# Moving the third reading of a VectorE exponential to GpSimd in a multi-query attention kernel, with a fourth buffer set and a new packing

## The chip, the cores and the metric

The kernel runs on one core of one Trainium2 chip. The metric is the device time of one execution in microseconds (us), the median of several. The engines are called PE (TensorE), ACT (ScalarE), DVE (VectorE) and POOL (GpSimd), as the profile has them; "spacing" is the time from one instruction's start to the next one's, and a "record" is the profile's own duration of one instruction. A tile is written as partitions x columns.

## The reference, cut to what matters

```python
S, D, H, Dh, F = 2048, 640, 32, 20, 1728          # bf16
xn = layernorm(x)
q = (xn @ wq) as 32 heads;  k = xn @ wk;  v = xn @ wv     # one k and one v for all heads
p = softmax(q k^T / sqrt(Dh));  o = p v
out = x + o @ wo + silu(xn @ w1) @ w2
```

The costly part is the exponential: 32 heads x 2048 x 2048 scores, which are 2048 blocks of 128 x 512.

Of the kernel before, what the change touches and what calls it, by code (L numbers as in the profile page):

```python
# [46 lines left out]
NZ = 3  # L47
ZB = 3
ZWAIT = 6
SWITCH = 0.105  # L50
S_LEAD = 0.56
PV_PRESS = 12
DVE_TH = 3.0
U_PRIO = 0.9
X_PRIO = 1.6
# [287 lines left out]
class Builder:  # L343
# [17 lines left out]
    def alloc(self):  # L361
        sb = self.sb
        self.ps = self.stack.enter_context(self.nc.psum_tensor("psall", [P, 8 * BANK], F32))
        self.xnT = sb([P, DC, S], BF16)
        self.w1 = sb([P, DC, F], BF16)
        self.w2 = sb([P, FC, D], BF16)
        self.wq = sb([P, DC, D], BF16)
        self.wqp = sb([P, DC, 2 * P], BF16)
        self.qd = sb([P, 2, QW], BF16)
        self.wo = sb([P, DC, D], BF16)  # L370
        self.kv_st = sb([P, 2, DC, DH], BF16)
        self.wk = sb([P, DC, P], BF16)
        self.kT = sb([P, 2, S], BF16)
        self.v = sb([P, 5, KT, SLOT], BF16)
        self.qT = sb([P, HT, 2, QW], BF16)
        self.E = sb([P, NBLK * QW], BF16)
        self.Z = sb([P, NZ, ZB * QW], I16)
        self.Y = sb([P, NZ, 2, ZB * QW], I16)
        self.U = sb([P, 2, QW], BF16)
        self.stk = sb([P, 64], BF16)  # L380
        self.UT = sb([P, 2, 4, P], BF16)
        self.W = sb([P, 4, 3, DH + 1], F32)
        self.hT = sb([P, FC, QW], BF16)
        self.o = sb([P, 2, 4, D], BF16)
        self.oT = sb([P, DC, QW], BF16)
        self.tb = sb([P, 2, QW], BF16)
        self.xres = sb([P, 4, D], BF16)
        self.yx = self.w1[:, :, :].rearrange("p a b -> p (a b)")[:, 0:8 * D].bitcast(F32).rearrange(
            "p (i e) -> p i e", i=4)
        self.ost = sb([P, 3, D], BF16)  # L390
        self.idf = self.w2[:, 4, 0:2 * P].bitcast(F32)
        self.idb = sb([P, P], BF16)
        self.st6 = sb([P, NT, 2, 6], F32)
        self.mv = sb([P, NT, 2], F32)
        self.rstd = sb([P, NT], F32)
        self.nb = sb([P, NT], F32)
        self.ex2 = sb([P, NT], F32)
        self.junk = self.E[:, (NBLK - 2) * QW:(NBLK - 2) * QW + D]
        self.tmp = sb([P, 4, NT], F32)
        self.rL = sb([P, 2, 4, 3], F32)  # L400
        self.offq = sb([P, 1], F32)
        self.offk = sb([P, 1], F32)
        self.eps = sb([P, 1], F32)
        self.zero = sb([P, 512], BF16)
        self.XS = 11
        hflat = self.hT[:, :, :].rearrange("p a b -> p (a b)")
        oflat = self.o[:, :, :, :].rearrange("p a b c -> p (a b c)")
        self.okeys = [("o", a, h) for a in range(2) for h in range(H)]

        def xslot(n):  # L410
            if n < self.XS:
                return hflat[:, n * D:(n + 1) * D]
            if n < NT - 1:
                return self.xres[:, n - self.XS, :]
            return oflat[:, DC * D:(DC + 1) * D]

        def xkeys(n):
            if n < self.XS:
                return [("hT_x", n)]
            if n < NT - 1:  # L420
                return [("xres", n - self.XS, 0), ("xres", n - self.XS, 1)]
            return [("x15",)] + self.okeys
        self.xslot = xslot
        self.xkeys = xkeys
# [7 lines left out]
    def steps_init(self):  # L432
# [26 lines left out]
        self.nqd = 0  # L459
        self.y_done = {}  # L460
# [16 lines left out]
    def bank_for_job(self):  # L477
        if not self.started:
            banks = [7, 6, 5, 4, 3]
        elif not self.pv_started:  # L480
            banks = [7, 6]
        else:
            banks = [7]
# [23 lines left out]
    def job_ready(self, job):  # L507
        if job.gate is not None and not job.gate():
            return INF
        if job.min_step > self.s_next:  # L510
            return INF
        r = self.reads_ready(job.reads)
        if r == INF:
            return INF
        return max(r, self.bank_for_job()[0])
# [32 lines left out]
    def step(self, now):  # L548
# [82 lines left out]
        else:  # L631
            if job is None:
                job = cand.popleft()
                job.bank = self.bank_for_job()[1]
# [94 lines left out]
    def do_S(self, t, now):  # L729
# [42 lines left out]
        if dv:  # L772
# [9 lines left out]
            sc.new("dve", t_dve_ps(QW), p1, [("B", bb)], [("Z", zs, zp)], prio=1.0, name=f"p1_{t}")  # L782
        first = kt == 0
# [27 lines left out]
        self.pv_wait.append((pv, dv))  # L811
        if dv:
# [16 lines left out]

    def flush_z(self):  # L830
# [7 lines left out]
        for k in range(2):  # L838
# [19 lines left out]
        tail = None  # L858
        if self.pv_wait[-1][0].kt == KT - 1:
            tail = self.pv_wait.pop()  # L860
        seen = False
        hosts = []
        for op, _ in self.pv_wait:
            seen = seen or op is first
            if seen and op.after is not None and not op.after and op.kt < KT:
                hosts.append(op)
        while ts and hosts and len(ts) % 3 == 1:
            th, key, kt = ts.pop()
            op = hosts.pop()
            op.after.append(th)  # L870
            op.mm += 1
            op.deps |= sc.deps_of([key], ())
            sc.readers[key].append(op)
        while ts:
            part = ts[:3]
            ts = ts[3:]
# [8 lines left out]
            op.kt = part[-1][2]  # L885
# [5 lines left out]
        self.zblocks = []  # L891

    def norm_dma(self, g, rows):
# [23 lines left out]
        for c in sorted(set(x // H for x in us)):  # L917
            js = [j for j, x in enumerate(us) if x // H == c]
            h0, m = us[js[0]] % H, len(js)
            dst = self.o[:, c % 2, :, h0 * DH:(h0 + m) * DH].rearrange("p q (i d) -> p q i d", d=DH)  # L920
# [4 lines left out]
                dst, src, rb, ALU.mult), [("W", 0), ("W", 1), ("rL", up)], [("o", c % 2, h0 + i) for i in range(m)],  # L925
# [4 lines left out]
    def end_group(self, g):  # L930
# [34 lines left out]
        for c in sorted(set(x // H for x in us)):  # L965
# [7 lines left out]
            for rq, hh in runs:  # L973
                m = len(rq)
                dst = self.o[:, c % 2, :, hh * DH:(hh + m) * DH].rearrange("p q (i d) -> p q i d", d=DH)
# [4 lines left out]
                    dst, src, rb, ALU.mult), [("UB",), ("rL", up)], [("o", c % 2, hh + i) for i in range(m)],  # L980
# [5 lines left out]
    def q_job(self, ht, act=False):  # L986
# [19 lines left out]
        reads = [("xnT", i) for i in range(4)] + [("wq", ht)]  # L1006
# [62 lines left out]
    def try_oT(self, c):  # L1069
# [6 lines left out]
        for i in range(4):  # L1076
            op = self.sc.dma("sp", lambda q, i=i: q.dma_start_transpose(
                self.oT[:, 0:nk, i * P:(i + 1) * P], self.o[:, c % 2, i, 0:nk * P]),
                [("o", c % 2, h) for h in range(need)], [("oT", i), ("oTv", c, i)], nk * P * P * 2,
# [4 lines left out]
    def oT_last_job(self, c):  # L1084
# [3 lines left out]
        for i in range(4):  # L1088
            def f(pe, b, i=i):
                return pe.transpose(self.bk16(b)[:, i * P:(i + 1) * P], self.o[:, c % 2, i, k * P:(k + 1) * P],  # L1090
# [6 lines left out]
        reads = [("o", c % 2, h) for h in range(H)] + [("idb",)]  # L1097
# [121 lines left out]
    def prologue(self):  # L1219
# [58 lines left out]
        pool(0.7, lambda g: g.memset(self.wk[:, :, :], 0.0), [], [("wk",)])  # L1278
        wqd = self.wqp[:, :, :].rearrange("p c (h j) -> p c h j", j=SLOT)
        wqs = self.wq[:, :, 0:160].rearrange("p c (h d) -> p c h d", d=DH)  # L1280
        for kk in range(2):
            pool(0.4, lambda g, kk=kk: g.memset(wqd[:, :, 4 * kk:4 * kk + 4, DH:SLOT], 0.0), [], [("wq", kk)])
# [28 lines left out]
        def wkrep(a):  # L1311
            dst = self.wk[:, :, :].rearrange("p c (r j) -> p c r j", j=SLOT)[:, :, :, 0:DH]
            s = self.kv_st[:, 0, :, :]
            src = bass.AP(self.kv_st, s.offset, [list(s.ap[0]), list(s.ap[1]), [0, 4], [1, DH]])
# [37 lines left out]
        oflat = self.o[:, :, :, :].rearrange("p a b c -> p (a b c)")  # L1352
# [78 lines left out]
        for par in range(2):  # L1431
            for ht in range(2 if par == 0 else 0, HT):
                np_("dve", 0.31, lambda v, par=par, ht=ht: v.tensor_scalar(
                    self.qT[:, ht, par, :], self.zero[:, 0:QW], self.offq[:, :], None, ALU.add),
                    [("zero",), ("offq",)], [("qb", par, h) for h in range(4 * ht, 4 * ht + 4)],
# [23 lines left out]
        def k_job(j):  # L1459
# [20 lines left out]
            return Job(f"kv{j}", mms, [("xnT", 2 * j), ("xnT", 2 * j + 1), ("wk",)], consume)  # L1480
# [99 lines left out]
```

## The kernel before: what the change and the argument touch

A list scheduler in Python lays out every instruction when the program is built, with its own table of durations. The chip then follows that fixed order on each engine, and semaphores carry only the data dependences.

The kernel makes 688 steps. In a step PE writes up to three blocks of scores into PSUM. ACT takes the exponential of two or three of them in one instruction. In most steps DVE takes the third by a bit trick: it clamps the scaled scores into int16 (`p1`), and those 16 bits, read as bf16, are a coarse exponential. Two more "readings" of the same bits, shifted by 43 and by 86, are weighted into the sum by PE and make it accurate.

```python
PH = ((0, 1.0), (43, 0.8046875), (86, 0.625))      # shift, weight of the three readings
...
def p1(v):                                          # L780: one block, PSUM -> int16
    return v.tensor_scalar(self.Z[:, zs, zp * QW:(zp + 1) * QW], self.bk(bb), 0.0, ZMAX, ALU.max, ALU.min)
...
for k in range(2):                                  # L839: up to three blocks at a time
    sc.new("dve", t_dve_4x(w), lambda v, k=k: v.tensor_scalar(
        self.Y[:, zs, k, 0:n * QW], Z, float(PH[k + 1][0]), None, ALU.add), zk, ...).lock = True
...
def want_dve(self, t):                              # does DVE get a block in this step?
    ...                                             # back: DVE's backlog in the schedule
    return back < DVE_TH                            # 3.0 us
```

`lock` keeps the scheduler from laying a marked DVE instruction and a marked GpSimd instruction over each other. GpSimd, in this kernel, normalises finished outputs and little more.

The softmax here doesn't subtract the row's maximum and nothing guards it: scores larger than these inputs give would overflow.

## Time and profile before

| | before |
|---|---|
| time, median | 749.49 us (749.35 to 750.24, 3 runs; 749.66 with the fourth that was run beside the changed kernel) |
| busy: PE, DVE, ACT, POOL | 713.0, 709.2, 709.3, 105.6 us of 747.3 |
| blocks on DVE, of 688 steps | 603 |
| granted clock of PE | 0.997 |

Busy shares of PE, DVE and ACT are alike and do not tell which one bounds. The prediction below reads the single groups and stretches. Two lines of the page's second part (the span in 40 slices; a digit is tenths of busy time or of full clock):

```profile
POOL 5421111010111111111011111101011100101100
PEclk9999999999999999999999999999999999999999
```

GpSimd is idle nearly nine tenths of the time after the prologue (it is busy 72.8 of the 600 us that the prediction shows), and the clock is nearly full throughout.

### The profile page before, as it was taken

How to read it: one execution, taken by the hardware profiler on the slowest of the kernel's cores; microseconds unless marked ns; L12 is line 12 of the kernel's file. 1: busy time of each engine (PE TensorE's matmuls, PEld its weight loads, DVE VectorE, ACT ScalarE, POOL GpSimd, SP SyncE). 2: the span in 40 equal slices, each digit the busy share in tenths (PEclk: the TensorE clock that was granted, in tenths of full speed). 3: DMA queues.
4: the chain of work that ended last, by engine and by line, in shares of the span. 5: the costliest groups of instructions: out<-in, count | busy, mean ns of one | idle time of the engine just before them, and what ended most of it. 6: DMA issues, size and time to landing. Idle time of an engine off the chain costs nothing.

```text
span 747.3 us, 17758 instructions
## 1 busy us (share of the span) xinstructions
PE 713.0 (95%) x6724; PEld 230.7 (31%) x6779; DVE 709.2 (95%) x1390; ACT 709.3 (95%) x780; POOL 105.6 (14%) x280
## 2 busy tenths in 40 slices
PE   8889999999999999999999999999999999999996
PEld 4332222233323322223333332222333332223342
DVE  7889999999999999999999999999999999999987
ACT  7879999999999999999999999999999999999952
POOL 5421111010111111111011111101011100101100
PEclk9999999999999999999999999999999999999999
DMA  6570000000012211000002211000002110000011
GB/s 188 148 264 16 21 15 15 18 13 15 16 23 54 58 33 22 10 8 8 9 9 43 58 40 34 14 8 8 9 8 51 42 47 8 15 9 8 9 36 36
DMA packets 55962, 27.06 MB, mean 36 GB/s; under 512 B 43686, under 2 KB 55238, under 8 KB 55878
## 3 DMA queue, kind: packets, MB, share of 16 engines
q1 hardware_dynamic: 54566, 25.87, 13.4%
q8 instruction: 55, 0.90, 0.5%
q10 hardware_dynamic: 1312, 0.05, 0.1%
q14 instruction: 29, 0.24, 0.1%
HBM read 11.36 MB, written 2.62 MB: 19 GB/s over the span
## 4 chain that ended last, share of the span: by engine, by line
PE 51%; ACT 22%; DVE 15%; issue 6%; DMA 2%; POOL 2%; SPq 0%; DVEq 0%; ACTq 0%; POOLq 0%
ACT sbt L766 20%; PE psall L748 17%; PE psall L827 17%; PE psall L1112 8%; DVE sbt L780 7%; DVE sbt L839 4%; PE psall L1050 3%; ACT sbt L1058 3%; PE psall L1117 3%; DMA sbt<-sbt 2%; PE psall L1016 2%; PE psall L672 1%; DVE sbt L938 1%; DVE sbt L1023 0%; DVE sbt L1063 0%
## 5 line engine op out<-in xcount | busy, mean ns | idle before, releaser
L766 ACT ACTIVATE sbt<-psall 128x1024 bf16<-128x1024 f32 (+2 forms) x688 | 676.8, 1130 | 21.1 <-PE psall L748 15.7
L780 DVE TENSOR_SCALAR sbt<-psall 128x512 int16<-128x512 f32 x603 | 403.0, 683 | 15.0 <-PE psall L748 11.9
L748 PE MATMUL psall<-sbt 32*128 32x512 bf16 x2048 | 269.0, 385 | 14.1 <-ACT sbt L766 9.0
L827 PE MATMUL psall<-sbt 128*32 128x512 bf16 x3428 | 263.7, 384 | 1.7 <-DVE sbt L938 1.3
L839 DVE TENSOR_SCALAR sbt<-sbt 128x1536 int16<-128x1536 int16 (+2 forms) x434 | 220.0, 528 | 1.8
L748 PEld LDWEIGHTS psall<-sbt 32*128 32x128 bf16 x2048 | 68.7, 91 | 253.8 <-ACT sbt L766 123.6
L827 PEld LDWEIGHTS psall<-sbt 128*32 128x32 bf16 x3428 | 67.7, 94 | 111.5 <-issue 67.2
L908 POOL CAST sbt<-sbt 128x168 f32<-128x168 bf16 x42 | 15.2, 361 | 546.4 <-DMA sbt<-sbt 546.4
L1112 PE MATMUL psall<-sbt 128*128 128x320 bf16 x448 | 85.8, 302 | 0.1
L1050 PE MATMUL psall<-sbt 128*128 128x512 bf16 (+1 forms) x246 | 75.9, 384 | 4.6 <-issue 2.4
L1112 PEld LDWEIGHTS psall<-sbt 128*128 128x128 bf16 x448 | 34.8, 97 | 43.6 <-issue 33.0
L1063 DVE SCALAR_TENSOR_TENSOR sbt<-sbt,psall 128x512 bf16<-128x512 bf16 (+1 forms) x56 | 38.0, 679 | 3.1 <-PE psall L748 2.0
L1058 ACT ACTIVATE sbt<-psall 128x512 bf16<-128x512 f32 (+1 forms) x56 | 38.6, 689 | 0.0
L924 POOL TENSOR_TENSOR sbt<-sbt 128x240 bf16<-128x240 f32 (+2 forms) x44 | 26.7, 608 | 46.1 <-DVE sbt L915 46.1
L1117 PE MATMUL psall<-sbt 128*128 128x320 bf16 x160 | 31.3, 303 | 1.2 <-DVE sbt L1095 0.7
L1050 PEld LDWEIGHTS psall<-sbt 128*128 128x128 bf16 (+1 forms) x280 | 19.2, 98 | 41.5 <-issue 26.7
L938 DVE CAST sbt<-psall 128x512 bf16<-128x512 f32 x43 | 29.4, 683 | 1.4 <-PE psall L827 1.3
L910 POOL TENSOR_TENSOR sbt<-sbt 128x44 f32<-128x44 f32 x84 | 26.2, 312 | 6.6
L1016 PE MATMUL psall<-sbt 128*128 128x512 bf16 (+1 forms) x78 | 24.7, 384 | 2.3 <-issue 1.7
L672 PE MATMUL psall<-sbt 128*32 128x512 bf16 (+7 forms) x78 | 23.6, 353 | 0.0
L685 PE MATMUL psall<-sbt 128*128 128x512 bf16 (+4 forms) x67 | 18.2, 412 | 2.2 <-POOL sbt L1276 1.4
L1117 PEld LDWEIGHTS psall<-sbt 128*128 128x128 bf16 x160 | 12.1, 97 | 17.2 <-issue 9.7
(85 smaller groups left out, 198.6 us busy)
## 6 DMA issues: line engine op xcount, KB each, us to landing
sbt<-in_A_x_dram SPq DMA_DIRECT2D x32, 160.0 KB, 3.5
out_dram<-sbt SPq DMA_DIRECT2D x16, 160.0 KB, 1.8
sbt<-in_B_w_dram SPq DMA_DIRECT2D x5, 432.0 KB, 5.3
sbt<-sbt SPq DMA_DIRECT2D x105, 20.0 KB
sbt<-in_B_w_dram SPq DMA_DIRECT2D x13, 160.0 KB, 3.9
sbt<-sbt SPq DMA_TRANSPOSE x67, 2.4
sbt<-in_A_wo_dram SPq DMA_DIRECT2D x5, 160.0 KB, 6.2
sbt<-in_A_wq_dram SPq DMA_DIRECT2D x5, 140.0 KB, 3.7
```

The lines of the kernel that those rows point to most:

```text
L748: ins = pe.matmul(self.bk(par3 + j), self.kT[r:r + SLOT, kk, kt * P:(kt + 1) * P], self.qT[r:r + SLOT, h // 4, (x // H) % 2, :], start=Tru ...
L766: return a.activation(self.E[:, b0 * QW:(b0 + na) * QW], self.ps[:, par3 * BANK:(par3 + na) * BANK], AF.Exp, scale=ACT_SCALE)
L780: return v.tensor_scalar(self.Z[:, zs, zp * QW:(zp + 1) * QW], self.bk(bb), 0.0, ZMAX, ALU.max, ALU.min)
L827: return pe.matmul(self.bk(UBANK, 0, QW, q * SLOT, (q + 1) * SLOT), self.v[:, w, kt, :], x, start=start, stop=stop, tile_position=(0, q * ...
L839: sc.new("dve", t_dve_4x(w), lambda v, k=k: v.tensor_scalar(self.Y[:, zs, k, 0:n * QW], Z, float(PH[k + 1][0]), None, ALU.add), zk, [("Y", ...
L938: return v.tensor_copy(self.U[0:rows, up, :], self.bk(UBANK, 0, QW, 0, rows))
L1016: return pe.matmul(self.bk(b, 0, QW, 0, rows), self.wq[:, k, lo:hi], self.xnT[:, k, c * QW:(c + 1) * QW], start=(k == 0), stop=(k == DC - 1))
L1050: return pe.matmul(self.bk(b, 0, QW, 0, rows), self.w1[:, k, fk * P:fk * P + rows], self.xnT[:, k, c * QW:(c + 1) * QW], start=(k == 0), s ...
L1058: sc.new("act", t_act(QW), lambda a: a.activation(t, src, AF.Tanh, scale=0.5), [("B", b)], [("tb", tp)], prio=X_PRIO, name=f"th{c}_{fk}")
L1063: sc.new("dve", t_dve_ps(QW), lambda v: v.scalar_tensor_tensor(out=self.hT[0:rows, fk, :], in0=t, scalar=1.0, in1=src, op0=ALU.add, op1=AL ...
L1112: return pe.matmul(self.bk(b, 0, 320), self.hT[0:rows, fk, i * P:(i + 1) * P], self.w2[0:rows, fk, e0:e0 + 320], start=(m == 0), stop=(m = ...
L1117: return pe.matmul(self.bk(b, 0, 320), self.oT[:, k, i * P:(i + 1) * P], self.wo[:, k, e0:e0 + 320], start=(m == 0), stop=(m == tot - 1))
```

## The change

The intent is to take the reading shifted by 86 off the busy DVE and give it to the idle GpSimd, one block at a time; a fourth set of buffers lets GpSimd lag. Third readings that do not fill a PE pass of three are now kept over to the next set or put singly into column tiles that are free in steps without a DVE block. Priorities are retuned. Space for the fourth set comes from aliases and from one `o` buffer in place of two.

```diff
-NZ = 3
+NZ = 4
+Y_RATE = 1.3e-3
+Y_POOL = True
-PV_PRESS = 12
+PV_PRESS = 8
-U_PRIO = 0.9
-X_PRIO = 1.6
+U_PRIO = 1.1
+X_PRIO = 0.8
...
+            self.y_on_pool = self.y_pool(t)
+            if self.y_on_pool:
+                sc.new("pool", 0.12 + Y_RATE * QW, lambda v: v.tensor_scalar(
+                    self.Y[:, zs, 1, zp * QW:(zp + 1) * QW], self.Z[:, zs, zp * QW:(zp + 1) * QW], float(PH[2][0]), 0.0,
+                    ALU.add, ALU.add), [("Z", zs, zp)], [("Y", zs, 1, zp)], prio=4.0, name="yp").lock = True
...
-        for k in range(2):
+        for k in range(1 if self.y_on_pool else 2):
...
+        if self.thirds and self.can_host(pv):
+            self.host(pv, self.thirds.pop(0))
...   (packing of thirds rewritten; o reduced to one buffer; wqp, wk, kv_st laid into oT, ost, U; the rest of the diff is left out)
```

More of the change, by code (lines that the diff above doesn't have):

```diff
@@ L367, in alloc @@
         self.wq = sb([P, DC, D], BF16)
-        self.wqp = sb([P, DC, 2 * P], BF16)
         self.qd = sb([P, 2, QW], BF16)
         self.wo = sb([P, DC, D], BF16)
-        self.kv_st = sb([P, 2, DC, DH], BF16)
-        self.wk = sb([P, DC, P], BF16)
         self.kT = sb([P, 2, S], BF16)
@@ L379, in alloc @@
         self.U = sb([P, 2, QW], BF16)
+        self.kv_st = self.U[:, 1, 0:2 * DC * DH].rearrange("p (a c d) -> p a c d", a=2, c=DC)
         self.stk = sb([P, 64], BF16)
@@ L383, in alloc @@
         self.hT = sb([P, FC, QW], BF16)
-        self.o = sb([P, 2, 4, D], BF16)
+        self.o = sb([P, 4, D], BF16)
         self.oT = sb([P, DC, QW], BF16)
+        self.wqp = self.oT[:, :, :].rearrange("p c e -> p (c e)")[:, 0:DC * 2 * P].rearrange("p (c e) -> p c e", c=DC)
         self.tb = sb([P, 2, QW], BF16)
@@ L390, in alloc @@
         self.ost = sb([P, 3, D], BF16)
+        self.wk = self.ost[:, 2, :].rearrange("p (c e) -> p c e", c=DC)
         self.idf = self.w2[:, 4, 0:2 * P].bitcast(F32)
@@ L406, in alloc @@
         hflat = self.hT[:, :, :].rearrange("p a b -> p (a b)")
-        oflat = self.o[:, :, :, :].rearrange("p a b c -> p (a b c)")
-        self.okeys = [("o", a, h) for a in range(2) for h in range(H)]
+        oflat = self.o[:, :, :].rearrange("p b c -> p (b c)")
+        self.okeys = [("o", h) for h in range(H)]
         def xslot(n):
@@ L414, in xslot @@
                 return self.xres[:, n - self.XS, :]
-            return oflat[:, DC * D:(DC + 1) * D]
+            return oflat[:, 3 * D:4 * D]
         def xkeys(n):
@@ L459, in steps_init @@
         self.nqd = 0
+        self.thirds = []
         self.y_done = {}
@@ L475, in more, with bank_for_job @@
                 or self.cur_job is not None)
-    def bank_for_job(self):
-        if not self.started:
+    def bank_for_job(self, job=None):
+        if not self.started and (job is None or job.name[0] != "v"):
             banks = [7, 6, 5, 4, 3]
@@ L514, in job_ready @@
             return INF
-        return max(r, self.bank_for_job()[0])
+        return max(r, self.bank_for_job(job)[0])
     def s_reads(self, t, dv):
@@ L633, in step @@
                 job = cand.popleft()
-                job.bank = self.bank_for_job()[1]
+                job.bank = self.bank_for_job(job)[1]
                 self.cur_job = job
@@ L828, in pv_mm, with y_pool @@
                          tile_position=(0, q * SLOT), skip_group_check=True)
+    def y_pool(self, t):
+        return Y_POOL
     def flush_z(self):
@@ L857, in flush_z @@
         first = self.zblocks[0][1]
-        tail = None
-        if self.pv_wait[-1][0].kt == KT - 1:
-            tail = self.pv_wait.pop()
+        end = self.pv_wait[-1][0].kt == KT - 1
+        tail = self.pv_wait.pop() if end else None
         seen = False
-        hosts = []
         for op, _ in self.pv_wait:
             seen = seen or op is first
-            if seen and op.after is not None and not op.after and op.kt < KT:
-                hosts.append(op)
-        while ts and hosts and len(ts) % 3 == 1:
-            th, key, kt = ts.pop()
-            op = hosts.pop()
-            op.after.append(th)
-            op.mm += 1
-            op.deps |= sc.deps_of([key], ())
-            sc.readers[key].append(op)
-        while ts:
-            part = ts[:3]
-            ts = ts[3:]
+            if seen and self.can_host(op) and ts:
+                self.host(op, ts.pop())
+        if end and self.can_host(tail[0]) and len(self.thirds + ts) % 3 == 1:
+            self.host(tail[0], ts.pop() if ts else self.thirds.pop())
+        self.thirds += ts
+        while len(self.thirds) >= 3 or (end and self.thirds):
+            part = self.thirds[:3]
+            self.thirds = self.thirds[3:]
             def fn(pe, part=part):
@@ L884, in flush_z @@
             op.mm = len(part) + len(part) // 3
-            op.kt = part[-1][2]
+            op.kt = max(x[2] for x in part)
             op.na = 0
@@ L891, in flush_z, with can_host, host @@
         self.zblocks = []
+    def can_host(self, op):
+        return op.after is not None and not op.after and op.kt < KT
+    def host(self, op, third):
+        th, key, kt = third
+        op.after.append(th)
+        op.mm += 1
+        op.deps |= self.sc.deps_of([key], ())
+        self.sc.readers[key].append(op)
     def norm_dma(self, g, rows):
@@ L919, in norm_dma @@
             h0, m = us[js[0]] % H, len(js)
-            dst = self.o[:, c % 2, :, h0 * DH:(h0 + m) * DH].rearrange("p q (i d) -> p q i d", d=DH)
+            dst = self.o[:, :, h0 * DH:(h0 + m) * DH].rearrange("p q (i d) -> p q i d", d=DH)
             src = w[:, :, js[0]:js[0] + m, 0:DH]
@@ L924, in norm_dma @@
             sc.new("pool", 0.15 + 4 * m * DH * 0.00186, lambda v, dst=dst, src=src, rb=rb: v.tensor_tensor(
-                dst, src, rb, ALU.mult), [("W", 0), ("W", 1), ("rL", up)], [("o", c % 2, h0 + i) for i in range(m)],
+                dst, src, rb, ALU.mult), [("W", 0), ("W", 1), ("rL", up)], [("o", h0 + i) for i in range(m)],
                 prio=0.5, name=f"nrm{g}").lock = True
@@ L974, in end_group @@
                 m = len(rq)
-                dst = self.o[:, c % 2, :, hh * DH:(hh + m) * DH].rearrange("p q (i d) -> p q i d", d=DH)
+                dst = self.o[:, :, hh * DH:(hh + m) * DH].rearrange("p q (i d) -> p q i d", d=DH)
                 src = xv[:, :, rq[0]:rq[0] + m, 0:DH]
@@ L979, in end_group @@
                 op.after.append(sc.new("dve", t_dve_ps(4 * m * DH), lambda v, dst=dst, src=src, rb=rb: v.tensor_tensor(
-                    dst, src, rb, ALU.mult), [("UB",), ("rL", up)], [("o", c % 2, hh + i) for i in range(m)],
+                    dst, src, rb, ALU.mult), [("UB",), ("rL", up)], [("o", hh + i) for i in range(m)],
                     prio=U_PRIO, name=f"nrm{g}"))
@@ L1005, in consume @@
                        [("B", b), ("offq",)], ks, prio=X_PRIO, name=f"qev0_{ht}")
-        reads = [("xnT", i) for i in range(4)] + [("wq", ht)]
+        reads = [("xnT", i) for i in range(4)] + [("wq", ht)] + [("oT", i) for i in range(4)]
         return Job(f"q0_{ht}", mms, reads, consume, width=QW)
@@ L1077, in try_oT @@
             op = self.sc.dma("sp", lambda q, i=i: q.dma_start_transpose(
-                self.oT[:, 0:nk, i * P:(i + 1) * P], self.o[:, c % 2, i, 0:nk * P]),
-                [("o", c % 2, h) for h in range(need)], [("oT", i), ("oTv", c, i)], nk * P * P * 2,
+                self.oT[:, 0:nk, i * P:(i + 1) * P], self.o[:, i, 0:nk * P]),
+                [("o", h) for h in range(need)], [("oT", i), ("oTv", c, i)], nk * P * P * 2,
                 sem=self.s_oT[i], name="oTd")
@@ L1089, in f @@
             def f(pe, b, i=i):
-                return pe.transpose(self.bk16(b)[:, i * P:(i + 1) * P], self.o[:, c % 2, i, k * P:(k + 1) * P],
+                return pe.transpose(self.bk16(b)[:, i * P:(i + 1) * P], self.o[:, i, k * P:(k + 1) * P],
                                     self.idb[:, :])
@@ L1096, in consume @@
                    [("B", b)], [("oT", i) for i in range(4)] + [("oTl",)], prio=X_PRIO, name="oTl")
-        reads = [("o", c % 2, h) for h in range(H)] + [("idb",)]
+        reads = [("o", h) for h in range(H)] + [("idb",)]
         return Job("oTl", mms, reads, consume, gate=lambda: self.norm_made[c] == H)
@@ L1277, in prologue @@
         pool(0.1, lambda g: g.memset(self.eps[:, :], EPS), [], [("eps",)])
-        pool(0.7, lambda g: g.memset(self.wk[:, :, :], 0.0), [], [("wk",)])
+        pool(0.7, lambda g: g.memset(self.wk[:, :, :], 0.0), [], [("wk",), ("ost", 2, 0), ("ost", 2, 1)])
         wqd = self.wqp[:, :, :].rearrange("p c (h j) -> p c h j", j=SLOT)
@@ L1281, in prologue @@
         for kk in range(2):
-            pool(0.4, lambda g, kk=kk: g.memset(wqd[:, :, 4 * kk:4 * kk + 4, DH:SLOT], 0.0), [], [("wq", kk)])
+            pool(0.4, lambda g, kk=kk: g.memset(wqd[:, :, 4 * kk:4 * kk + 4, DH:SLOT], 0.0), [],
+                 [("wq", kk)] + [("oT", i) for i in range(4)])
         iv = self.idf[:, :].rearrange("p (r j) -> p r j", j=SLOT)[:, :, DH:DH + 2]
@@ L1313, in wkrep @@
             s = self.kv_st[:, 0, :, :]
-            src = bass.AP(self.kv_st, s.offset, [list(s.ap[0]), list(s.ap[1]), [0, 4], [1, DH]])
+            src = bass.AP(self.U, s.offset, [list(s.ap[0]), list(s.ap[1]), [0, 4], [1, DH]])
             return a.activation(dst, src, AF.Copy)
@@ L1350, in mvk @@
             return [("mv", n) for n in range(a, b_)]
-        oflat = self.o[:, :, :, :].rearrange("p a b c -> p (a b c)")
+        oflat = self.o[:, :, :].rearrange("p b c -> p (b c)")
         def xa(n):
@@ L1434, in prologue @@
                     self.qT[:, ht, par, :], self.zero[:, 0:QW], self.offq[:, :], None, ALU.add),
-                    [("zero",), ("offq",)], [("qb", par, h) for h in range(4 * ht, 4 * ht + 4)],
+                    [("zero",), ("offq",), ("mv", 3)], [("qb", par, h) for h in range(4 * ht, 4 * ht + 4)],
                     prio=6.0 + par, name="qz")
@@ L1479, in consume @@
                                                                  ALU.mult), [("wo",)], [("wo",)], prio=2.0)
-            return Job(f"kv{j}", mms, [("xnT", 2 * j), ("xnT", 2 * j + 1), ("wk",)], consume)
+            return Job(f"kv{j}", mms, [("xnT", 2 * j), ("xnT", 2 * j + 1), ("wk",), ("ost", 2, 0), ("ost", 2, 1)], consume)
         def v_job(n0, n1):
```

## The prediction

> **What bounds the kernel now.** I read the page first, then the groups of instructions by form, then busy time by stretch, then the timeline of single engines. The page puts three engines level, which says little:
>
> ```profile
> PE 713.0 (95%) x6724; PEld 230.7 (31%) x6779; DVE 709.2 (95%) x1390; ACT 709.3 (95%) x780; POOL 105.6 (14%) x280
> ```
>
> GpSimd (POOL) is the only engine with room. The stretch from 100 to 700 us, without prologue and tail, separates the others:
>
> ```profile
> core 0: us, PE busy (x) PEld busy (x) DVE busy (x) ACT busy (x) POOL busy (x), PEclk, DMA share, GB/s
> 100.00:700.00 600.00, 581.87 (x5595) 181.07 (x5635) 581.84 (x1085) 597.39 (x642) 72.78 (x187) 1.00 0.10 23
> ```
>
> ScalarE (ACT) is busy 597.4 of 600 us. The clock is full, so no difference is to be sought there. What fills ACT and VectorE (DVE) is in the groups by form:
>
> ```profile
> L766 ACT ACTIVATE sbt<-psall 128x1024 bf16<-128x1024 f32 x591 | 565.1, 1090 | 11.7 <-PE psall L748 6.4 <-PE psall L827 4.9
> L780 DVE TENSOR_SCALAR sbt<-psall 128x512 int16<-128x512 f32 x603 | 403.0, 683 | 15.0 <-PE psall L748 11.9
> L839 DVE TENSOR_SCALAR sbt<-sbt 128x1536 int16<-128x1536 int16 x346 | 188.9, 559 | 1.7
> L766 ACT ACTIVATE sbt<-psall 128x1536 bf16<-128x1536 f32 x83 | 124.1, 1503 | 0.8 <-PE psall L748 0.8
> L839 DVE TENSOR_SCALAR sbt<-sbt 128x1024 int16<-128x1024 int16 x80 | 31.8, 419 | 0.1
> ```
>
> The kernel makes 688 steps of up to three 128x512 score blocks. In 603 steps DVE takes one block (L780, then two "readings" of it, L839) and ACT does two (1090 ns); otherwise ACT does all three (1503 ns). A block moved from ACT to DVE is therefore worth 1503 - 1090 = 413 ns of ACT and no more.
>
> Records overlap their neighbours, so I take costs from start to start:
>
> ```profile
> 335.87 4.84 ACT L766 ACTIVATE sbt<-psall 128x1024 bf16<-128x1024 f32 x5
> 340.38 0.66 ACT L1058 ACTIVATE sbt<-psall 64x512 bf16<-64x512 f32 x1
> 340.86 4.25 ACT L766 ACTIVATE sbt<-psall 128x1024 bf16<-128x1024 f32 x4
> ```
>
> ```profile
> 400.39 0.55 DVE L839 TENSOR_SCALAR sbt<-sbt 128x1536 int16<-128x1536 int16 x1
> 400.85 0.68 DVE L780 TENSOR_SCALAR sbt<-psall 128x512 int16<-128x512 f32 x1
> 401.45 0.55 DVE L839 TENSOR_SCALAR sbt<-sbt 128x1536 int16<-128x1536 int16 x1
> 401.92 0.22 DVE L915 RECIPROCAL sbt<-sbt 128x12 f32<-128x12 f32 x1
> ```
>
> Two-block exp: (340.38 - 335.87)/5 = 0.90 us; tanh 0.48; three-block exp 0.90 + 0.41 = 1.32. DVE: L780 0.60, a three-block reading 0.46. In 100 to 700 us the stretches of L766 and L780 alone count 596 steps, 527 of them with a DVE block (share f = 0.884), so a step takes 600/596 = 1.007 us. ACT needs 0.884x0.90 + 0.116x1.32 + 46 tanh x 0.48/596 = 0.986 us of it, 98%. DVE needs 527x0.60 + 372 readings x about 0.45 + some 85 us of other work = 570 us, 95%. **ACT bounds the steady state**, and what could relieve it, a larger f, is barred by DVE being nearly full.
>
> **What the Trainium skill says.**
> - "SBUF — State Buffer", section "Who interferes with whom": a VectorE tensor_scalar in a 2-port mode and any GpSimd instruction take one shared port pair as an exclusive lock for the whole instruction, and the later one blocks. The trace agrees: comparing record by record, the three-block L839 averages 551 ns without a GpSimd record beside it and 591 ns (worst 881) with one; L905 on GpSimd goes from 343 to 519 ns. By the same section L780, with PSUM input, takes no lock.
> - "GPSIMD Engine Reference", section 3.1: elementwise work near 1 cycle per element, with a 512-element loop measured at 769 ns. Here a 256-column GpSimd tensor_scalar (L1473) takes 0.47 us and an unblocked 640-column one (L1478) 0.73; interpolated, 512 columns are 0.64, and 0.72 with the 0.08 us between dependent ones. No int16 instance is in this trace, so 0.72 to 0.79 is my estimate.
> - "Perfetto Trace Analysis", section "GPSIMD Engine Instruction": trust spacing, not spans. I do so where neighbours exist.
>
> **The change part by part.**
> *Third reading to GpSimd.* It removes half of the 434 L839 instructions, 217. Of these about 173 are three-block at 0.466, 40 two-block at 0.334, 4 single: 81 + 13 + 1 = 95 us less DVE, or 0.14 us per step. By itself this moves nothing, since ACT is the bound. It pays only as added DVE blocks. Such a block now costs DVE 0.60 + 0.155 = 0.755 us.
> *Where the added blocks stop.* If every step had one, DVE would need 0.755 + about 0.15 = 0.905 us per step and ACT 0.90 + 0.04 = 0.94: both would allow some 0.96 us a step (-5%, 715 us). The third claimant is the shared port: per DVE block 0.72 to 0.79 on GpSimd and 0.16 of the remaining reading on DVE, plus GpSimd's normalisation chain per group of 16 steps, 0.33 + 0.34 + 0.27 + 0.26 + 0.59 = 1.79 us, or 0.11 per step. At f = 1 that is 0.99 to 1.06 us: more than the 0.96 wanted. So **the port, hardly used before, caps f.** The kernel's order is fixed when it is built: its list scheduler gives DVE a block only while DVE's backlog is below 3 us, charges GpSimd 0.12 + 0.0013x512 = 0.786 us per block (a constant in the diff) and never lets the two lock holders overlap. At 97% port use and ACT at 98%, f(0.786 + 0.155) + 0.11 = 0.97 x (1.36 - 0.42f)/0.98, so f = 0.91 and the step is 0.998 us. At 95% f comes to about 0.89, at 100% 0.93.
> *Arithmetic.* 0.91 of 688 is 626 blocks, 23 more than 603: 23 x 0.413 = 9.5 us off ACT. That is the main term.
> *Fourth Z/Y set, thirds carried over.* They let GpSimd lag by a set without stopping L780. I see only the 15.0 us idle ahead of L780, mostly waiting for scores, so at most 1 or 2 us of direct gain; the set is what makes the lag bearable.
> *Single thirds in free column tiles.* 3428 - (1445 + 2x603) = 777 third-matmuls today. Packing them better saves perhaps ten TensorE passes of 0.22 us: 2 us on an engine that, by start-to-start spacing, has about 7% idle and some 3% filler matmuls. Not on the path: 0.
> *Priorities (evacuations after L780, tanh and output work before it), pressure 8 for 12.* Order only; plus or minus 2 us.
> *Aliased buffers, one o buffer.* The transposes of o must be done before the next chunk's first normalisation, about 16 steps later; the aliases of oT, ost, U delay some prologue work. Plus 0 to 2 us.
> Sum: 749.5 - 9.5 - 1.5 + 1 = about 739.5; I put 739.
>
> **The rivals.**
> (a) *The port is no obstacle.* If nearly every step got its block (f 0.97), 64 x 0.413 = 26 us would go: 723. For it: GpSimd is at 14%, DVE gets 95 us back, and the 0.64 us interpolation is below the 0.786 charged. Against it: the order is fixed by the charged number, not by the real one.
> (b) *GpSimd or its lock becomes the bound on the chip.* If an int16 block took 0.90 us, f = 0.91 would need 0.91x1.06 + 0.11 = 1.07 us per step: 6% longer, about 790. Milder: each of some 215 remaining readings waits on average 0.2 us for a GpSimd instruction, 43 us of DVE; with DVE at 0.84 us per step this still fits in 0.998, but some L780 come late, scores wait for banks, and ACT loses a per cent: 747. The 591 against 551 ns speaks for the mild form.
> (c) *TensorE takes over.* At 0.998 us per step it keeps some 6% idle and filler it can drop: no.
> (d) *ACT is unblocked but nothing changes*: if the scheduler, held by the lock, keeps f at 0.885, 748.
>
> **Range and chances.** Centre 739, between (d) or mild (b) above and (a) below: 724 to 753. The 2% lines are 734.5 and 764.5. Crossing 734.5 needs some 36 more blocks or fewer ACT stalls than now; my cap at 100% port use gives 0.93x688 = 640 blocks, 37 more, so it is the edge of what I think possible: one in three. Slower by 2% needs the strong (b): 6%.
>
> **What the new profile would show.** Right if: L839 falls to about 210 and a GpSimd tensor_scalar of 128x512 int16 appears some 626 times, with spacing of 0.7 to 0.8 us; GpSimd is busy 70 to 80%; DVE busy falls below 93% in 100 to 700 us while ACT stays at 98% or more; three-block exps fall from 83 to about 60; the mean of the remaining three-block L839 rises above 0.56 us with the lock. Wrong if: the number of L780 is above 645 (rival a) or below 612 (d); the GpSimd block is over 0.85 us and TensorE waits for it at L827 (b); or time moves in the prologue or tail, before 100 or after 700 us, where I expect under 2 us.

## The result, and the profile after

The changed kernel takes **1325.43 us** (1324.96 to 1326.67, 4 runs) against 749.66 us. The ratio is 1.768, 95% interval 1.765 to 1.771. (A ratio here is the mean time of one kernel's runs over that of the other's in the same rounds, so not quite the ratio of the medians.) The prediction said 739 us, 724 to 753.

First the page's head and slices of the changed kernel:

```profile
PE 906.6 (68%) x6809; PEld 243.5 (18%) x6809; DVE 685.0 (52%) x1196; ACT 737.8 (56%) x780; POOL 1290.0 (97%) x901
...
POOL 5899999999999999999999999999999999999996
PEclk9876786778678788877867777887866767678685
```

GpSimd is full from the third slice to the last but one; every other engine has fallen to half or two thirds. The clock of PE has dropped to 0.768. The stretch from 100 to 700 us, for which the prediction showed ACT at 597 of 600 us, now reads (length, then busy PE, PEld, DVE, ACT, POOL, clock, DMA share, GB/s):

```profile
100.00:700.00 600.00, 401.10 (x3079) 102.48 (x3076) 302.90 (x496) 339.74 (x348) 599.29 (x399) 0.77 0.05 11
```

GpSimd fills 599.3 us of it, and ACT only 339.7: the bound has moved.

The groups by form (busy us, mean ns, then idle time before them) name the instruction:

```profile
L788 POOL TENSOR_SCALAR sbt<-sbt 128x512 int16<-128x512 int16 x621 | 1200.6, 1955 | 2.7 <-DVE sbt L783 2.2
L769 ACT ACTIVATE sbt<-psall 128x1024 bf16<-128x1024 f32 x605 | 597.7, 1029 | 488.5 <-PE psall L751 482.2 <-PE psall L837 3.7
L783 DVE TENSOR_SCALAR sbt<-psall 128x512 int16<-128x512 f32 x621 | 419.8, 685 | 267.4 <-PE psall L751 246.8 <-POOL sbt L788 7.8 <-POOL sbt L1496 2.1
L852 DVE TENSOR_SCALAR sbt<-sbt 128x1536 int16<-128x1536 int16 x185 | 129.5, 705 | 1.0
L769 ACT ACTIVATE sbt<-psall 128x1536 bf16<-128x1536 f32 x67 | 96.6, 1456 | 45.4 <-PE psall L751 45.2
```

L788 is the new instruction. It takes 1955 ns on average; the prediction had 720 to 790. GpSimd was idle before it for 2.7 us in all, so its queue hardly ever empties. ACT, which bounded the kernel before with hardly any idle time, now stands idle 488.5 + 45.4 us, waiting for scores. The number of blocks (621 on L783) is close to the 626 predicted, and ACT's instructions are as quick as before.

The spacing, from GpSimd's timeline, confirms the duration:

```profile
600.03 1.92 POOL L788 TENSOR_SCALAR sbt<-sbt 128x512 int16<-128x512 int16 x1
601.92 0.26 POOL L927 TENSOR_TENSOR sbt<-sbt 128x40 f32<-128x40 f32 x1
602.15 1.92 POOL L788 TENSOR_SCALAR sbt<-sbt 128x512 int16<-128x512 int16 x1
604.04 0.59 POOL L941 TENSOR_TENSOR sbt<-sbt 128x240 bf16<-128x240 f32 x1
```

601.92 - 600.03 = 1.89 us of GpSimd per block. So 621 blocks are 621 x 1.89 = 1174 us, more than the whole time before. The chain of work that ended last (shares of the span by engine), and then who waited for whom (us in total, times, longest), give the path by which it reaches ACT:

```profile
POOL 35%; issue 8%; PE 7%; DVE 3%; DMA 1%; POOLq 0%; DVEq 0%
```

```profile
ACT sbt L769 <- PE psall L751: 540.6, 300, 11.4
PEld psall L837 <- POOL sbt L788: 271.4, 116, 6.3
DVE sbt L932 <- POOL sbt L927: 263.0, 40, 11.9
DVE sbt L783 <- PE psall L751: 246.8, 242, 7.2
PEld psall L751 <- DVE sbt L783: 238.1, 177, 10.4
```

PE takes the weighted sums in a fixed order, so a third reading that is late holds the sums behind it (second line, up to 6.3 us). In the same fixed order DVE waits for GpSimd's normalisation, which is stuck in the same queue, before the reciprocal (third line, up to 11.9 us), and every later `p1` stands behind that. Then PSUM banks are not freed, scores are not written, and ACT waits. Where the time came from is thus plain. What the trace alone doesn't say is why the instruction takes 1.89 us.

### The profile page after: what moved, and what is told of

It is laid out like the page before. It is cut to its first block, busy times and chain, and to the rows that moved or that the text cites. A ratio compares the mean times of both kernels' runs of the same rounds, so it can differ in the third digit from the quotient of the medians.

```text
span 1324.9 us, 18814 instructions
## 1 busy us (share of the span) xinstructions
PE 906.6 (68%) x6809; PEld 243.5 (18%) x6809; DVE 685.0 (52%) x1196; ACT 737.8 (56%) x780; POOL 1290.0 (97%) x901
## 4 chain that ended last, share of the span: by engine, by line
POOL 35%; issue 8%; PE 7%; DVE 3%; DMA 1%; POOLq 0%; DVEq 0%
POOL sbt L788 33%; PE psall L751 2%; PE psall L837 2%; DVE sbt L783 1%; PE psall L1129 1%; POOL sbt L927 1%; POOL sbt L941 1%; PE psall L1067 1%; POOL sbt L922 1%; POOL sbt L925 1%; DVE sbt L852 1%; PE psall L1134 0%; DMA sbt<-sbt 0%; POOLq L1537 0%; DVE sbt L1152 0%
## 5 line engine op out<-in xcount | busy, mean ns | idle before, releaser
L788 POOL TENSOR_SCALAR sbt<-sbt 128x512 int16<-128x512 int16 x621 | 1200.6, 1955 | 2.7 <-DVE sbt L783 2.2
L769 ACT ACTIVATE sbt<-psall 128x1024 bf16<-128x1024 f32 (+2 forms) x688 | 697.9, 1061 | 547.5 <-PE psall L751 540.6
L783 DVE TENSOR_SCALAR sbt<-psall 128x512 int16<-128x512 f32 x621 | 419.8, 685 | 267.4 <-PE psall L751 246.8
L837 PE MATMUL psall<-sbt 128*32 128x512 bf16 x3463 | 333.4, 459 | 256.4 <-POOL sbt L788 224.5
L751 PE MATMUL psall<-sbt 32*128 32x512 bf16 x2048 | 319.0, 458 | 140.5 <-DVE sbt L783 137.1
L852 DVE TENSOR_SCALAR sbt<-sbt 128x1536 int16<-128x1536 int16 (+2 forms) x222 | 148.1, 678 | 1.1
L932 DVE RECIPROCAL sbt<-sbt 128x12 f32<-128x12 f32 x42 | 9.6, 229 | 263.0 <-POOL sbt L927 263.0
L1067 PE MATMUL psall<-sbt 128*128 128x512 bf16 (+1 forms) x280 | 102.5, 459 | 9.7 <-DVE sbt L1080 9.7
L1129 PE MATMUL psall<-sbt 128*128 128x320 bf16 x448 | 108.6, 359 | 0.7 <-DVE sbt L1146 0.6
L1134 PE MATMUL psall<-sbt 128*128 128x320 bf16 x160 | 41.7, 379 | 1.2 <-DVE sbt L1112 0.6
L1033 PE MATMUL psall<-sbt 128*128 128x512 bf16 (+1 forms) x95 | 38.0, 497 | 0.0
L675 PE MATMUL psall<-sbt 128*32 128x512 bf16 (+8 forms) x66 | 23.6, 431 | 0.0
```

What stands on the lines that cost most here:

```text
L751: ins = pe.matmul(self.bk(par3 + j), self.kT[r:r + SLOT, kk, kt * P:(kt + 1) * P], self.qT[r:r + SLOT, h // 4, (x // H) % 2, :], start=Tru ...
L769: return a.activation(self.E[:, b0 * QW:(b0 + na) * QW], self.ps[:, par3 * BANK:(par3 + na) * BANK], AF.Exp, scale=ACT_SCALE)
L788: sc.new("pool", 0.12 + Y_RATE * QW, lambda v: v.tensor_scalar(self.Y[:, zs, 1, zp * QW:(zp + 1) * QW], self.Z[:, zs, zp * QW:(zp + 1) * Q ...
L837: return pe.matmul(self.bk(UBANK, 0, QW, q * SLOT, (q + 1) * SLOT), self.v[:, w, kt, :], x, start=start, stop=stop, tile_position=(0, q * ...
L852: sc.new("dve", t_dve_4x(w), lambda v, k=k: v.tensor_scalar(self.Y[:, zs, k, 0:n * QW], Z, float(PH[k + 1][0]), None, ALU.add), zk, [("Y", ...
L1033: return pe.matmul(self.bk(b, 0, QW, 0, rows), self.wq[:, k, lo:hi], self.xnT[:, k, c * QW:(c + 1) * QW], start=(k == 0), stop=(k == DC - 1))
```

## The experiments

Three answers were possible for the 1.89 us: the int16 type, the port shared with DVE, or the pair of operations (add, add). A fourth possibility was that another part of the change carried some of the loss. Where a time is given from one run, it has no interval. The median of the kernel before was 749.7 to 750.2 us beside all of them.

### e1_y_off: everything but the move

```diff
-Y_POOL = True
+Y_POOL = False
```

> The whole change except that the third reading stays on VectorE (fourth set, single thirds, priorities, aliased buffers all kept). Theory A (the GpSimd block, 1.89 us start to start, 621 times, is the whole loss): about 749.5 + (603 - 594) x 0.413 = 753 us, range 747 to 760, clock back at 1.00. Rival D (another part of the change, such as the priorities or the shared buffers, or the lower TensorE clock as a cause, carries a good part of the loss): above 900 us.

747.11 us, ratio 0.9954 (0.9940 to 0.9969), clock 0.995. The whole loss is in the moved reading. The rest even gains 3 us, although the build gives DVE nine blocks fewer, so my 753 was too high. The clock is back as well, so its fall came with the slow reading. This run doesn't separate the two; that the clock isn't what bounds follows from GpSimd, which is busy 97% of the changed kernel's span.

### e2_bf16_view: the type changed

```diff
-  self.Y[...], self.Z[...], 86.0, 0.0, ALU.add, ALU.add
+  self.Y[...].bitcast(BF16), self.Z[...].bitcast(BF16), 86.0, 0.0, ALU.add, ALU.add
```

> Same instruction on GpSimd, same order, same size and op pair, but the 16-bit words are read and written as bf16 instead of int16 (result wrong on purpose). Theory A (the element type int16 is what costs): spacing falls from 1.89 to 0.65 to 0.75 us, GpSimd about 75% busy, kernel 730 to 755 us. Rival B (the shared port: VectorE's instructions hold GpSimd up, whatever the type): spacing stays near 1.9 us and the kernel near 1325. Rival C (the pair add, add is slow): also near 1.9 us.

1329.87 us, result wrong. The group by form:

```profile
L788 POOL TENSOR_SCALAR sbt<-sbt 128x512 bf16<-128x512 bf16 x621 | 1202.8, 1961 | 2.6 <-DVE sbt L783 2.1
```

Hardly different: 1961 ns for 1955. My first theory, that int16 is what costs, fell here.

### e3_mult_add: the operations changed

```diff
-  86.0, 0.0, ALU.add, ALU.add
+  1.0, 86.0, ALU.mult, ALU.add
```

> int16 kept, the op pair changed from (x + 86) + 0 to (x * 1) + 86, result right. Theory A: unchanged, 1.89 us and about 1325 us. Rival C (op pair): 0.65 to 0.75 us a block and 730 to 755 us. Rival B: unchanged too.

744.00 us (one run), correct.

```profile
L788 POOL TENSOR_SCALAR sbt<-sbt 128x512 int16<-128x512 int16 x621 | 412.6, 664 | 129.2 <-DVE sbt L783 62.2 <-PE psall L837 20.1 <-PE psall L751 5.0
```

The same order of work, the same type, the same 621 blocks: 664 ns in place of 1955, and GpSimd is now idle 129 us before these blocks. Written as (x * 1) + 86 the sum costs about a third of what it costs as (x + 86) + 0; by spacing, back to back, 0.70 us against 1.89. The port is excluded as well: DVE is given the same instructions in the same order in both kernels, and the 395 slow blocks of the changed kernel with no DVE reading (L852) beside them still took 1.92 us.

### e4_int32_pairs: two values in one word

```diff
-  v.tensor_scalar(Y, Z, 86.0, 0.0, ALU.add, ALU.add)
+  v.tensor_tensor(Y.bitcast(I32), Z.bitcast(I32), y2c broadcast over 256, ALU.add)   # y2c = 86 * 65537
```

> Two int16 at a time as one int32: tensor_tensor add of a constant 86*65537 over 256 words, result exact because no sum passes 32767. Same order of all other work (621 blocks). Theory A in its narrow form (16-bit integers are slow, 32-bit integer add is native): 0.55 to 0.7 us a block like the 240-column tensor_tensor at 0.56, kernel 730 to 750 us. Theory A in its wide form (every integer type costs 3.6 ns per element): 256 x 3.6 + 0.05 = 0.97 us, GpSimd 675 us busy, kernel 750 to 790. Rival B: near 1325.

741.54 us, ratio 0.9886 (0.9869 to 0.9902), correct. A record without a DVE reading beside it takes 0.612 us, and the spacing back to back is 0.57. Integer type and word size are no obstacle. "GPSIMD Engine Reference" of the Trainium skill, section 4.1, says that a GpSimd tensor_tensor add with inputs and output all of one 32-bit integer type is exact; the correct result of this run agrees.

### f1_add_alone, f2_add_mult, f3_add_max, i1_mult_alone, i2_mult_max: which operations

Each is the changed kernel with one edit: `86.0, None, add`; `86.0, 1.0, add, mult`; `86.0, 0.0, add, max`; `1.0, None, mult`; `1.0, 86.0, mult, max`. The last two are wrong.

> The third reading as one add with no second op, the form VectorE uses for its own readings; int16, same order, result right. Theory P (only the pair add, add is slow): 0.6 to 0.75 us a block, 738 to 750 us. Theory Q (an add of an immediate as first op is slow): 1.7 to 1.9 us and above 1250 us. Theory R (two ops are what is slow unless the first is a multiply): fast like P.

> (x + 86) * 1, result right. Theory P: 0.6 to 0.75 us and 738 to 750 us (the prologue's add, mult on 256 columns took 0.47 us, though with its first operand from a tile). Theory Q: 1.9 us and 1325. Theory R: 1.9 us and 1325.

> (x + 86) max 0, result right. If whatever has no multiply is slow on GpSimd: 1.5 to 1.9 us a block, 1070 to 1325 us. If only the lone add and the pair add, add are slow: 0.62 us and 741 to 745 us.

> GpSimd writes x * 1 with no second op (the third reading is then unshifted: result wrong on purpose). If a multiply anywhere makes the instruction fast: 0.62 us a block, 741 to 745 us. If it is the pair of two ops with a multiply in it (in the kernel before, the lone multiply L1405 took 248 ns on 4 columns, the pair mult, add L1398 194 ns): about 1.4 to 1.5 us like the lone add, 1040 to 1080 us.

> (x * 1) max 86 on GpSimd, result wrong on purpose. If a multiply is enough: 0.62 us and 741 to 745 us. If only pairs made of a multiply and an add or a second multiply are fast: 1.8 to 1.9 us and about 1320 us.

All rows but that of the change are single runs. The spacing is the median between two such blocks in a row.

| operations on GpSimd, 128x512 int16 | median record, us | spacing, us | kernel, us |
|---|---|---|---|
| mult, add (e3) | 0.62 | 0.70 | 744.0 |
| add, mult (f2) | 0.62 | 0.70 | 742.4 |
| add alone (f1) | 1.49 | 1.46 | 1071.9 |
| mult alone (i1) | 1.49 | 1.46 | 1068.6 |
| add, add (the change) | 1.92 | 1.89 | 1325.4 |
| add, max (f3) | 1.92 | 1.88 | 1323.5 |
| mult, max (i2) | 1.92 | 2.00 | 1408.8 |

The lone add, in the group by form:

```profile
L788 POOL TENSOR_SCALAR sbt<-sbt 128x512 int16<-128x512 int16 x621 | 944.2, 1543 | 3.4 <-DVE sbt L783 3.0
```

All three theories that I put forward for f1 fell in some run: a lone add is not fast (f1, against P and R), and an add first is not in itself slow (f2, against Q). That a multiply is enough, which came next, fell in i1 and i2. What the runs leave is narrower and stranger: the fast forms are pairs made of a multiply and an add, in either order (and perhaps multiply, multiply: L1478 of the kernel before took 0.73 us for 640 columns, in bf16 and not in int16). One operation alone is slower than such a pair, and other pairs are slower still. In add, add and in add, max the second number was 0 in every run; whether that number matters was not tried. Why the forms differ no run shows.

i2 is 85 us slower than f3 at the same record. Three of its blocks in a row, from GpSimd's timeline:

```profile
598.56 5.91 POOL L788 TENSOR_SCALAR sbt<-sbt 128x512 int16<-128x512 int16 x3
```

That is (5.91 - 1.92) / 2 = 2.00 us from start to start, where f3 has 1.88: after a block of i2 some 0.08 us pass before the next begins, and in f3 the two overlap by 0.03. (5.91 is from the first start to the last end.) From start to start, the 621 blocks take 67 us more than in f3, and GpSimd's other instructions 17 more, which is nearly the whole difference. e3 and f2 have the same gap of 0.08 us: their blocks cost 0.70 us and not 0.62. The Trainium skill, "Perfetto Trace Analysis", section "GPSIMD Engine Instruction", says to time GpSimd instructions by spacing and not by their spans; this agrees, since equal records of 1.92 us hide 67 us here.

### f4_two_halves: per column or per instruction

```diff
-  one tensor_scalar of 512 columns (add, add)
+  two tensor_scalar of 256 columns (add, add)
```

> The pair add, add kept, each block in two instructions of 256 columns. If its cost is per element (3.6 ns each): two of 0.95 to 1.0 us, kernel 1325 to 1400 us. If it is a fixed 1.2 us per instruction on top of 0.7: two of 1.5 to 1.6 us, kernel about 2000 us.

1453.04 us; the spacing is 1.035 us for 256 columns against 1.889 for 512. That is (1889 - 1035) / 256 = 3.34 ns per column and 0.18 us per instruction: mostly per column, so larger instructions would have saved little.

### e6_one_set_in_4: throughput or latency

```diff
-        return Y_POOL
+        return self.zset == 0        # and Y_RATE = 3.46e-3, the slow form's true cost
```

> The slow pair add, add kept, but only one set in four on GpSimd (142 blocks, charged 1.89 us in the schedule; VectorE 564 blocks). GpSimd then needs 142 x 1.89 + 72 = 340 us. If GpSimd's throughput is what made the changed kernel slow: no more loss than fewer blocks give, 747 + 30 x 0.413 = 759, range 752 to 775. If the 1.9 us latency of a block itself hurts (TensorE waiting for each third): above 800.

763.95 us (one run), inside the range for throughput, with 564 blocks on DVE. Against e1 that is 16.8 us for 30 blocks fewer, of which 12.4 at 0.413 us each; where the other 4.4 come from no run shows. So a slow reading that GpSimd has time for doesn't ruin the kernel, but it isn't shown to be free.

### g_ma_113 and g_i32_090: what limits the fast forms

```diff
-Y_RATE = 1.3e-3
+Y_RATE = 1.13e-3      # g_ma_113, on e3: 637 blocks
+Y_RATE = 0.9e-3       # g_i32_090, on e4: 652 blocks
```

> The multiply-add form, with the scheduler's charge set to what the chip took (0.12 + 0.00113 x 512 = 0.70 us instead of 0.786); it then gives VectorE 637 blocks instead of 621. If my cap by the shared port was right and only the charge limits: 16 x 0.413 = 6.6 us less than the 744.0 of e3, so 737, range 733 to 741. If lock waits on the chip eat it: 744 or above.

> The int32-pair form with a charge of 0.58 us a block, below the 0.61 the record shows; 652 blocks. If blocks are still worth 0.413 us each: 741.5 - 31 x 0.413 = 729. If the shared port is what limits on the chip, as g_ma_113 hinted (16 blocks more, no gain): 738 to 746, with more GpSimd and VectorE records stretched by each other and ACT below 97% by its own need.

g_ma_113: 743.08 us, ratio 0.9900 (0.9864 to 0.9935). g_i32_090: **736.05 us**, ratio 0.9807 (0.9786 to 0.9827), correct; it beats both kernels, by 1.9% against the kernel before (by the 2% rule of the record its verdict is "unclear"). Its stretch from 100 to 700 us (length, then busy PE, PEld, DVE, ACT, POOL, clock, DMA share, GB/s):

```profile
100.00:700.00 600.00, 583.35 (x5756) 180.47 (x5803) 565.50 (x979) 593.57 (x655) 449.39 (x772) 1.00 0.11 24
```

The charge in the scheduler, not GpSimd's idle time, sets the number of blocks, as predicted: 604, 621, 637, 652 at a rate of 1.5, 1.3, 1.13 and 0.9 ns per column (the first only built, not run). But blocks added this way are worth less than 0.413 us each. From e4 to g_i32_090 31 blocks brought 5.5 us, not 12.8; from e3 to g_ma_113 16 blocks brought 0.9, and with one run of e3 not even that is certain. Meanwhile the part of 100 to 700 us in which ACT had nothing of its own to do (600 less the instructions that start there, at their spacings of 0.904, 1.330 and 0.477 us) grew from 13.9 us in e4 to 19.9.

### h1_before_plus_pool, i3_three_sets, i4_old_order: is the move enough by itself?

h1 is the kernel before with the fast reading on GpSimd and nothing else; i3 and i4 are e3 with one part undone.

```diff
+  (h1) sc.new("pool", 0.786, ... tensor_scalar(Y, Z, 1.0, 86.0, ALU.mult, ALU.add)); the DVE loop over k in range(1)
-  (i3) NZ = 4
+  (i3) NZ = 3
-  (i4) PV_PRESS = 8;  U_PRIO = 1.1; X_PRIO = 0.8
+  (i4) PV_PRESS = 12; U_PRIO = 0.9; X_PRIO = 1.6
```

> The kernel before with one part of the change alone, in the fast form: the third reading block by block on GpSimd as (x * 1) + 86; three sets, old packing, old priorities. The build gives VectorE 627 blocks. If the moved reading is what gains: 749.9 - 24 x 0.413 = 740, range 738 to 745, like e3 and f2. If it needs the fourth set and the rest (e1 alone gave 3 us): 745 to 752.

> e3 (mult, add) with three Z and Y sets instead of four; the build then gives VectorE 646 blocks instead of 621. If sets do not matter on the chip, only blocks: 744 - 25 x 0.413 = 734, range 731 to 738. If the fourth set is what the kernel before lacked when it lost time with GpSimd readings (h1, 756.8): 750 to 757, with ScalarE idle for TensorE of 20 us and more.

> e3 with the old pressure and priorities (12, 0.9, 1.6) and four sets; 614 blocks. If the order is what the kernel before lacked: 750 to 757 us. If order is worth nothing: 744 + 7 x 0.413 = 747, range 743 to 749.

h1: 756.77 us, ratio 1.0087 (1.0070 to 1.0104). i3: 775.54 us, ratio 1.0338 (1.0322 to 1.0353). i4: 750.37 us, ratio 1.0006 (0.9989 to 1.0023). ACT's waits in e3 and then in i3 (us in total, times, longest):

```profile
ACT sbt L769 <- PE psall L751: 17.0, 16, 2.8
```

```profile
ACT sbt L769 <- PE psall L751: 55.8, 53, 2.3
```

With three sets ACT waits 39 us longer for scores, and the kernel loses 31.5 us against e3 (one run) although DVE has 25 blocks more (646). In this kernel the move needs its fourth set. By itself, as h1 shows, the move would have made the kernel slower even in its fast form. ACT's spare time from 100 to 700 us, counted as above, says the same: 13.4 us in the kernel before, 15.7 in e3, 26.4 in h1, 52.2 in i3. That h1, with three sets, loses less than i3 may lie in its order, its packing and its fewer blocks; no run separates that.

The old order costs 6.4 us, but not where ACT bounds. i4's last exponential ends earlier than that of e3 (723.7 us against 727.3), although it has seven blocks fewer (614). What follows it, the last output work, takes 23.9 us in i4 and 14.7 in e3. So the new order gained at the end of the kernel. What in the order does this was not tried.

## Why the prediction was wrong

**The step that failed** is the cost of a block on GpSimd: "No int16 instance is in this trace, so 0.72 to 0.79 is my estimate." It measured 1.89 us, and so GpSimd and not ACT became the bound. I took the risk for one of type and interpolated over columns; type costs nothing (e2), and I did not look at the operations. The two lines that I interpolated between, L1473 and L1478, are add-mult and mult-mult. The runs show add-mult to be of the fast kind (f2); mult-mult had no run of its own, but L1478's duration fits it. The new instruction is add-add. For the fast kind the interpolation was good: 0.64 us from the trace, and 0.72 with the gap between dependent blocks; e3 measured 0.62 and, by spacing, 0.70. The page of before held a weak warning, in GpSimd's groups by form:

```profile
L1398 POOL TENSOR_SCALAR sbt<-sbt 128x4 f32<-128x4 f32 x4 | 0.8, 194 | 0.4
L1405 POOL TENSOR_SCALAR sbt<-sbt 128x4 f32<-128x4 f32 x2 | 0.5, 248 | 0.2
L1383 POOL TENSOR_SCALAR sbt<-sbt 128x4 f32<-128x4 f32 x2 | 0.5, 233 | 7.3 <-DVE sbt L1335 7.2
```

L1398 is mult-add, L1405 a lone multiply, L1383 a lone add. On four columns the lone operations took longer than the pair. It is weak because an int32 mult-add, L1384, also took 250 ns, and each mean is of two to four records.

**Rival (b)** was the right mechanism with the wrong size: "GpSimd or its lock becomes the bound". Its own formula with the measured cost, 0.91 x (1.89 + 0.16) + 0.11 = 1.98 us per step, is near the 600/324 = 1.85 us that the trace shows from 100 to 700 us, in which 324 steps begin. Without the 0.16 for DVE's share of the port it is 1.83, nearer still: GpSimd's own queue bounds. I gave slower than 2% a chance of 6% because I let the strong form reach only 0.90 us a block. An instruction form that the trace doesn't contain deserved a wider range.

**The order is fixed at build time**, and so nothing could adapt: right, and worse than I made of it. The number of blocks was right (621 for 626), as were L852 at "about 210" (222) and three-block exps at "about 60" (67).

**The lock.** I said that the mean of the three-block reading would rise above 0.56 us: 705 ns in the changed kernel and 655 in e3, against 551 when nothing is beside it. Right. The two engines do slow each other: GpSimd's fast block goes from a mean of 0.62 to 0.75 us when a DVE reading overlaps it (e3). L783, with its PSUM input, stays at 685 ns beside a full GpSimd (683 before), as I took from the Trainium skill, "SBUF — State Buffer", section "Who interferes with whom". But that section also says that whoever comes second is blocked for the whole of the first one's instruction, and this the changed kernel doesn't show:

```profile
210.40 1.92 POOL L788 TENSOR_SCALAR sbt<-sbt 128x512 int16<-128x512 int16 x1
210.92 0.56 DVE L852 TENSOR_SCALAR sbt<-sbt 128x1536 int16<-128x1536 int16 x1
```

The reading runs wholly within the GpSimd block, and both take what they take alone. Of 122 three-block readings that lie within one GpSimd block, 71 took at most 570 ns. So the averages of 551 and 591 ns, with which I said that the trace agrees, show a slowing and not an exclusive lock. Nor was the lock the reason for the 1.89: 416 of the 621 slow blocks had no three-block reading beside them and averaged 1.92 us.

**The main term** looks as if it held once the operation was repaired: e3 and f2 take 744.0 and 742.4 us against my 739. That is partly luck. Measured against e1, the same kernel without the move (594 blocks, 747.1 us), the 27 blocks that the move adds brought 3.1 us in e3, 4.7 in f2 and 5.6 in e4, that is 0.12 to 0.21 us each and not 0.413. Part of the rest is seen as waiting: ACT's spare time from 100 to 700 us, counted as for g_i32_090, was 11.7 us in e1 and 15.7 in e3. Where all of it goes no run shows. And 2.8 us of the way to 739 came from parts that I had put at nothing (e1).

**The small terms were wrong.** For the fourth set I put 1 or 2 us, because DVE hardly waited before; i3, with everything else of the change in place, makes it over 31 us. I had looked at the waits of a kernel in which GpSimd held nothing up. For priorities and pressure I put plus or minus 2; i4 shows 6.4, and it is gained in the tail, where I expected under 2. The packing, the order and the rest, without the move, gained 2.8 us (e1) in spite of nine blocks fewer, where I had summed to about nothing.

**Small slips of the sums.** 596 steps counts instructions at the borders of stretches twice: 592 two- and three-block exps start from 100 to 700 us, which makes 1.014 us a step. Rival (b), 6% longer, is 796 us and not 790. Neither changes the argument.

## What to carry to other kernels

Before moving work to an engine, find in a trace the very instruction that will run there: engine, operation, both ALU operations, and size. A duration of the same opcode with other operations can be off by a factor of about three. In a kernel whose order is fixed when it is built, an engine that was idle and becomes the slowest drags the others at its pace; so measure the new instruction alone, or run the program once, before retuning anything around it. And don't take what a unit of work costs the slowest engine, here 0.413 us of ACT per block, for what its removal will bring: here it brought 0.12 to 0.21 us.

## What the Trainium skill lacked or had wrong

- "GPSIMD Engine Reference", section 3.1, makes the cost per element a matter of the number of operations and operands and of the form of the loop, and gives 769 ns for 512 elements. It does not say that tensor_scalar depends on which pair of operations it has, nor that one operation can cost more than two: on 128x512 int16 the record was 0.62 us for mult-add and add-mult, 1.49 for a lone add or multiply, 1.92 for add-add, add-max and mult-max. No page that I read has it.
- The same page, section 4.1, calls one-input elementwise work "roughly line-rate". The fast pairs took 0.70 us from start to start for 512 columns, but add-add took 3.34 ns per column plus 0.18 us (spacing of 256 and of 512 columns).
- "SBUF — State Buffer", section "Who interferes with whom", says that of a VectorE instruction in a 2-port mode and a GpSimd instruction the later one fully blocks. The three-block readings, which the prediction took to be in such a mode, don't show it: in the changed kernel 71 of the 122 whose records lie within one GpSimd block of some 1.9 us took at most 570 ns, against 551 alone. The section doesn't tell when the two can run side by side.
